# Decode attention with a gated MLP on one core: wo in another place of the key ring, the last loads placed and divided anew, exponentials put before copies

## The chip, the cores and the metric

The kernel runs on one core of a Trainium2 chip. The core has a matrix engine (PE, with its weight loads shown as PEld), a vector engine (DVE), a scalar engine (ACT), GpSimd (POOL) and a queue for loads (SP). Each of them works through its own list of instructions in order. Loads from memory (HBM) go through 16 DMA engines, which share out every load among them. The metric is the time of one execution on the device in microseconds (us).

## The reference

For a batch of 4 with one new token each, a layer norm of x feeds two branches, and their sum with x is the output (4 x 1 x 640, bf16).

```python
xn = layernorm(x)                                  # x: 4 x 1 x 640
q = (xn @ wq)                                      # 32 heads of 128
scores = einsum('bhqd,bhkd->bhqk', q, k_cache) * 128 ** -0.5
o = einsum('bhqk,bhkd->bhqd', softmax(scores), v_cache)   # 4096 keys
A = o.reshape(4, 1, 32 * 128) @ wo
z = gelu(xn @ w_in); z1, z2 = z[..., :864], layernorm(z[..., 864:])
B = (z1 * (w_sp * z2 + b_sp)) @ w_out
out = x + A + B
```

Each of the 4 x 32 heads has its own 4096 keys and values of 128 numbers. These two caches are nearly all of the 282 MB that are read.

## The kernel before

The attention is cut into 16 *units*. A unit `u` is 8 heads of one batch row: `hg, b = divmod(u, 4)`; four units make a group `hg`, which ends with a projection by 8 heads' rows of `wo` (1.31 MB). The keys of a unit are 8.39 MB, and so are its values. In on-chip memory they lie over 128 partitions, 16 partitions to a head.

**Places.** Keys live in a ring of seven places of 2.1 MB each (`ring`), four places to a unit. Units with an even number use places 3 to 6, odd ones 0 to 3 (`k_at`, L128); `k_order` (L129) says in which order a unit's four quarters are worked on, so that an odd unit begins with place 3. Values have one room of their own, `v_all`, for one unit. The exceptions are at the end: units 14 and 15 have their own places (L130, L131), the last unit's values go into places 0 to 3 of the ring when these are free (`VE_AT`), and `wo` of each group goes into one ring place (`WO_AT`, L132).

**Steps.** The loop over `n = 4 u + i` takes one quarter of keys per step:

- `product` (L487, DVE) multiplies the quarter by the unit's query, in place; `fold_half` (L493, DVE) adds its two halves.
- `sums` (L502, PE) adds further by 8 matmuls with an identity into PSUM; `row_sums` (L515, DVE) of the step before ends it. When `sums` is issued the place is given free (`busy.remove`, L509).
- In the first step of the next unit come `head_max` (L524 to L531, DVE: the maximum), `exps` (L537, ACT: the exponentials, with their sums) and `by_head` (L548, DVE: spreads them to a matrix `p_m` with zeros for the other heads).
- `weighted` (L572, PE, 64 matmuls) multiplies `p_m` by the values into `pv`; `take` (L584, ACT) copies `pv` to `o_rows`; `picked` (L603 or, in the last group, L650, PE) adds the rows that belong together.
- `weighted` and `take` of unit u stand in the second step of unit u+1 (`turns`, L662), of units 12 and 13 in the fourth step of the next unit (L663, L664); unit 14's comes after the loop.
- After a group: `group_turn` (DVE) and `group_proj` (L633, PE), which gives wo's place free.

**The loads' list.** `loads` (L167 to L175) is one list in a fixed order, each entry with the places it needs. `pump`, called at the end of every step, issues entries from the head of the list as long as their places are free, and stops at the first that isn't. SP then still waits, in order, for the engines that last read the place. So an entry whose place comes free late also holds all the entries behind it. In the middle the order is values of u, keys of u+2, and after every fourth unit wo; the end is (keys in halves):

```python
loads += [k_load(NU - 2, 0, 2), v_load(NU - 4), k_load(NU - 2, 2, 4), k_load(NU - 1, 0, 2)]
loads += [v_load(NU - 3), k_load(NU - 1, 2, 4), v_load(NU - 2)]
loads += [ve_load(0, (0, NC)), ve_load(1, V_CUTS), wo_load(HG - 1)]
```

The last unit's values come as one load for the first half and four of falling size for the second (`V_CUTS`), the last wo in five parts.

**The end.** After the loop: `weighted` and `take` of unit 14, the last row sums, maximum, `exps` and `by_head` of unit 15; the sum of the exponentials (L717); picks of unit 14; `weighted` of unit 15's first half; its copy and picks; 128 small matmuls (L732) for the second half; the division (L740), the projection by the last wo (L633), a copy (L746) and the store.

The order on PE, DVE, ACT and SP is the order in which the program issues the instructions. In this text K14 means the keys of unit 14, V14 its values, wo2 the wo of group 2.

Of the kernel before, what the change touches and what calls it, by code (L numbers as in the profile page):

```python
# [17 lines left out]
def kernel(  # L18
# [14 lines left out]
    nc = tc.nc  # L33
# [19 lines left out]
    NU = HG * Bsz  # L53
    NR = HT * S // P
    NK = 4
    HC = NR // NK
    NC = 2 * HC
    HD2 = Dh // 2
    RW = 8
    QW = HC * Dh  # L60
# [6 lines left out]
    NG = NR // CB  # L67
# [25 lines left out]
    v_all = places.tile([P, NK * QW], BF16, name="v_all")  # L93
# [22 lines left out]
    def run_of(cache, u):  # L116
        hg, b = divmod(u, Bsz)
        return cache[b, HT * hg : HT * (hg + 1)].rearrange("h s d -> (h s) d").rearrange(
            "(p c) d -> p (c d)", c=NR
        )  # L120
# [5 lines left out]
    k_at, k_order = {}, {}  # L126
    for u in range(NU):
        k_at[u] = [r if u % 2 else NK - 1 + r for r in range(NK)]  # L128
        k_order[u] = [NK - 1, 0, 1, 2] if u % 2 else [0, 1, 2, 3]  # L129
    k_at[NU - 2], k_order[NU - 2] = [4, 5, 0, 1], [0, 1, 2, 3]  # L130
    k_at[NU - 1], k_order[NU - 1] = [2, 3, 4, 5], [0, 1, 2, 3]  # L131
    VE_AT, WO_AT = (0, 2), 6  # L132

    def k_load(u, r0=0, r1=NK):
        at = k_at[u][r0:r1]

        def go():
            nc.sync.dma_start(
                out=ring[:, at[0] : at[0] + r1 - r0, :],
                in_=run_of(A_k_cache, u)[:, r0 * QW : r1 * QW].rearrange("p (r w) -> p r w", w=QW),  # L140
            )

        return go, at

    def v_load(u):
        def go():
            nc.sync.dma_start(out=v_all[:], in_=run_of(A_v_cache, u))

        return go, [V]

# [16 lines left out]
    loads = [k_load(0, 0, 2), (load_w, []), k_load(0, 2, 4), k_load(1)]  # L167
# [3 lines left out]
            loads.append(wo_load(u // Bsz))  # L171
    assert u + 2 == NU - 3
    loads += [k_load(NU - 2, 0, 2), v_load(NU - 4), k_load(NU - 2, 2, 4), k_load(NU - 1, 0, 2)]
    loads += [v_load(NU - 3), k_load(NU - 1, 2, 4), v_load(NU - 2)]
    loads += [ve_load(0, (0, NC)), ve_load(1, V_CUTS), wo_load(HG - 1)]  # L175
    busy = {V}
    n_loaded = [0]
# [10 lines left out]
    v_runs = v_all[:].rearrange("p (c d) -> p c d", d=Dh)  # L188
# [24 lines left out]
    for e in range(PAR):  # L213
        nc.gpsimd.tensor_copy(
            out=of_row[:, e, :, :, e, :],
            in_=ident[:].rearrange("p (k q) -> p q k", q=QD)[:, 0:Bsz, :, None].to_broadcast(
                [P, Bsz, NQ, LN]
            ),
# [15 lines left out]
    for i in range(NSTAT):  # L234
# [5 lines left out]
        out=rstd[:], in_=mv[:, 1:2], func=ACT.Sqrt, bias=eps_tile[:Bsz], scale=1.0  # L240
# [4 lines left out]
        out=xn_bf[:],  # L245
# [9 lines left out]
    for c in range(DC):  # L255
        nc.tensor.transpose(
            out=xnT_ps[:, c, :], in_=xn_v[:, c, :], identity=ident[:Bsz, :Bsz]
# [8 lines left out]
    for e in range(PAR):  # L266
        q_ps = ps_pv.tile([P, HG, Dh], FP32, tag="pv", name="q_ps")
        for c in range(DC):
            for k in range(NQ):
                nc.tensor.matmul(  # L270
                    out=q_ps[k * QD : (k + 1) * QD],
# [7 lines left out]
            out=rows[:], in0=q_ps[:], scalar1=scale_qk, scalar2=None, op0=ALU.mult  # L279
# [7 lines left out]
        out=hot[:].rearrange("p c h -> p (c h)"),  # L287
        in_=ident[:].rearrange("p (g m) -> p m g", m=QD),
# [6 lines left out]
        out=pick[:, :, Bsz - 1 :].rearrange("p c (k q) -> p c k q", q=QD)[  # L295
            :, :, :, 0 : PAR * Bsz : Bsz
        ],
# [236 lines left out]
    def exps(u):  # L534
        hg, b = divmod(u, Bsz)
        p_c[u] = small.tile([P, NR], BF16, name="p_c")
        nc.scalar.activation(  # L537
            out=p_c[u][:],
            in_=scores.pop(u)[:],
            func=ACT.Exp,  # L540
            bias=maxes.pop(u)[:],
            scale=1.0,
            accum_out=row_den[hg % NACC][:, b : b + 1],
        )

    def by_head(u):
        hg, b = divmod(u, Bsz)
        nc.vector.tensor_tensor(  # L548
            out=p_m[:, u % 2],
            in0=p_c.pop(u)[:].rearrange("p (g c) -> p g c", c=CB)[:, :, :, None].to_broadcast(  # L550
                [P, NG, CB, HT]
            ),
            in1=own[:, None, None, :].to_broadcast([P, NG, CB, HT]),
            op=ALU.mult,
        )
        if b == Bsz - 1:
            nc.vector.tensor_tensor(
                out=acc[hg % NACC][:, :, 0 : PAR * Bsz].rearrange("p k (e b) -> p k e b", b=Bsz),
                in0=row_den[hg % NACC][:, None, None, :].to_broadcast([P, NQ, PAR, Bsz]),
                in1=own[:].rearrange("p (e k) -> p k e", e=PAR)[:, :, :, None].to_broadcast(  # L560
                    [P, NQ, PAR, Bsz]
                ),
                op=ALU.mult,
            )

    def weighted(u, v_at, g0=0, more=False):
        n_g = v_at.shape[1] // CB
        if g0 == 0:
            pvs[u] = ps_pv.tile([P, GW], FP32, tag="pv", name="pv")
        for n in range(n_g):  # L570
            cg = n % CB
            nc.tensor.matmul(  # L572
                out=pvs[u][cg * QD : (cg + 1) * QD, :],
                lhsT=p_m[:, u % 2, g0 + n].rearrange("p c h -> p (c h)"),
                rhs=v_at[:, n * CB : (n + 1) * CB, :],
                start=(g0 == 0 and n < CB),
                stop=(not more and n >= n_g - CB),
            )
# [3 lines left out]
    def take(u):  # L582
        o = taken[u] = small.tile([P, CB, Dh], FP32, name="o_rows")
        nc.scalar.copy(out=o[:].rearrange("p c d -> p (c d)"), in_=pvs.pop(u)[:])  # L584
# [73 lines left out]
    def picked(u):  # L658
        (pick_last if u // Bsz == HG - 1 else pick_unit)(u)
# [7 lines left out]
    with tc.manual_schedule(engines={E.PE, E.DVE, E.Activation, E.SP}):  # L667
        stage_q(0)
        waiting = None
        mlp = gmlp()  # L670
        for n in range(NK * NU):
            u, i = divmod(n, NK)
            product(n)
            if n in (1, 2):
                next(mlp)
            if n:
                row_sums(n - 1)
            if i == 0 and u:
                head_max(u - 1)
                if waiting is not None:  # L680
                    picked(waiting)
            fold_half(n)
            if n == 1:
                next(mlp)
            if n in (1, 2):
                next(mlp)
            if i == 0 and u:
                exps(u - 1)
                by_head(u - 1)
            sums(n)  # L690
            if i == 0 and u + 1 < NU:
                stage_q(u + 1)
            if i == 0 and waiting is not None:
                if waiting % Bsz == Bsz - 1:
                    group_turn(waiting // Bsz)
                    group_proj(waiting // Bsz)
                waiting = None
            if n == 0:
                next(mlp)
            if n == 2:  # L700
                busy.remove(V)
            if n in turns:
                w = waiting = turns[n]
                if w % Bsz == Bsz - 1:
                    group_den(w // Bsz)
                weighted(w, v_runs)
                take(w)
                busy.remove(V)
            pump()
        weighted(NU - 2, v_runs)  # L710
        take(NU - 2)
        row_sums(NK * NU - 1)
        head_max(NU - 1)
        exps(NU - 1)
        by_head(NU - 1)
        den = ps_m.tile([P, NQ, PAR, Bsz], FP32, tag="m", name="den_all")
        nc.tensor.matmul(  # L717
            out=den[:],
            lhsT=ones_sq[:],
            rhs=acc[(HG - 1) % NACC][:, :, 0 : PAR * Bsz],  # L720
            start=True,
            stop=True,
        )
        rden = small.tile([P, NQ, PAR, Bsz], FP32, name="rden_all")
        nc.vector.reciprocal(out=rden[:], in_=den[:])
        picked(NU - 2)
        u, b = NU - 1, Bsz - 1
        weighted(u, v_ends[0])
        take(u)
        pick_last(u, more=True)  # L730
        for c in range(NC):
            nc.tensor.matmul(  # L732
                out=o_last[0][:, :, :, b],
                lhsT=v_ends[1][:, c, :],
                rhs=p_m[:, u % 2, NG // 2 + c // CB, c % CB, :].rearrange("p (e k) -> p k e", e=PAR),
                start=False,
                stop=(c == NC - 1),
            )
        o_n = small.tile([P, NQ, PAR, Bsz], BF16, name="o_n_last")
        nc.vector.tensor_tensor(out=o_n[:], in0=o_last[0][:], in1=rden[:], op=ALU.mult)  # L740
        gr[HG - 1] = [o_n[:, h % NQ, h // NQ, :] for h in range(HT)]
        group_proj(HG - 1)

        res = work.tile([P, NOH], BF16, name="res")
        out_v = out.flatten_outer_dims()
        nc.scalar.copy(out=res[0 : OG + Bsz], in_=out_ps[0 : OG + Bsz])  # L746
        nc.scalar.dma_start(out=out_v[:, 0:NOH], in_=res[0:Bsz])
        nc.sync.dma_start(out=out_v[:, NOH:D], in_=res[OG : OG + Bsz])
# [30 lines left out]
```

## Time and profile before

| what | us |
|---|---|
| median of three timed executions | 670.37 (669.91 to 671.1) |
| the profiled execution, its own time | 668.77 |
| span from its first to its last instruction | 667.0 |
| DVE busy | 522.5 (78%) |
| PE busy | 310.5 (47%) |
| ACT busy | 29.5 (4%) |
| DMA in the chain of waits | 61% of the span |
| mean granted clock of PE | 0.698 |
| read from memory | 282.24 MB, 423 GB/s over the span |

The page cuts the span into 40 slices and shows for each how busy every engine was, the granted clock of PE, the busy share of the DMA engines and the GB/s that they moved. The chain of waits follows the work that ended last back from the end: each line is a start, a length, and what it was (an engine and a line of the kernel, or a load in flight). The timeline of a queue shows when each load was issued. The table of windows gives busy time by engine for chosen stretches. The trace also keeps, for each load, a mark from every DMA engine that took part when its share was complete.

### The profile page before, as it was taken

Reading aid. Unit: us, or ns where it says so; the run is one execution under the profiler, and the core shown is the slowest. Engines: PE = TensorE matmul, PEld = TensorE weight load, DVE = VectorE, ACT = ScalarE, POOL = GpSimd, SP = SyncE. Lnnn points to the kernel's source line nnn. Section 1 sums busy time; section 2 is a strip of 40 time slices with the busy share of each in tenths; the row PEclk is TensorE's granted clock in tenths of the full one; section 3 lists DMA queues with packets and bytes.
Section 4 is the critical chain, followed back from the end, with each engine's and each line's share of the span. In section 5 each row is a group of like instructions: output and inputs, shape, how many; then the busy total and the mean of one; then the engine's idle time right before and its main releaser. Section 6 shows DMA issues by size and latency. Waiting matters only on the chain.

```text
span 667.0 us, 4615 instructions
## 1 busy us (share of the span) xinstructions
PE 310.5 (47%) x1999; PEld 136.1 (20%) x1999; DVE 522.5 (78%) x325; ACT 29.5 (4%) x73; POOL 2.7 (0%) x12
## 2 busy tenths in 40 slices
PE   0365372526336253552735255252653734646357
PEld 0131121112213121220212112021221311212125
DVE  2578978959697894969879596795969789997950
ACT  0020000000000000000000000000000000000000
POOL 1000000000000000000000000000000000000000
PEclk9756676766768686576767668576576866767685
DMA  9999999999999999999999999999999999999995
GB/s 376 421 465 436 425 429 421 433 440 440 429 436 402 451 432 432 437 436 436 433 429 422 409 424 441 436 437 436 436 437 436 405 436 398 415 459 436 401 414 221
DMA packets 8128, 282.54 MB, mean 424 GB/s; under 512 B 832, under 2 KB 1964, under 8 KB 3116
## 3 DMA queue, kind: packets, MB, share of 16 engines
q1 hardware_dynamic: 8088, 282.24, 98.5%
q8 instruction: 15, 0.25, 0.1%
q14 instruction: 5, 0.04, 0.0%
q10 hardware_dynamic: 20, 0.01, 0.0%
HBM read 282.24 MB, written 0.01 MB: 423 GB/s over the span
## 4 chain that ended last, share of the span: by engine, by line
DMA 61%; DVE 25%; PE 12%; issue 1%; ACT 0%; SPq 0%; DVEq 0%; ACTq 0%
DMA k_ring<-in_A_k_cache_dram 56%; DVE k_ring L487 13%; PE s_ps L502 7%; DVE k_ring L493 7%; DMA v_all<-in_A_v_cache_dram 5%; PE pv L572 3%; DVE s_sb L515 2%; DVE p_m L548 1%; DVE m L524 1%; PE out_ps L633 1%; PE o_last L650 1%; PE o_last L732 1%; DVE mt L526 0%; DVE mt L529 0%; DVE nm L531 0%
## 5 line engine op out<-in xcount | busy, mean ns | idle before, releaser
L487 DVE TENSOR_TENSOR k_ring<-k_ring,qbc 128x8192 bf16<-128x8192 bf16 x64 | 282.8, 4419 | 91.6 <-DMA k_ring<-in_A_k_cache_dram 91.6
L502 PE MATMUL s_ps<-k_ring,ident 128*128 128x512 bf16 x512 | 199.9, 561 | 316.4 <-DVE k_ring L493 316.3
L502 PEld LDWEIGHTS <-ident 128*128 128x128 bf16 x512 | 65.3, 130 | 429.7 <-issue 381.5
L493 DVE TENSOR_TENSOR k_ring<-k_ring 128x4096 bf16<-128x4096 bf16 x64 | 146.0, 2282 | 0.0
L572 PE MATMUL pv<-v_all,p_m 128*32 128x512 bf16 x960 | 60.5, 409 | 4.7 <-DMA v_all<-in_A_v_cache_dram 4.7
L515 DVE TENSOR_REDUCE s_sb<-s_ps 128x64 f32<-128x512 f32 x64 | 43.8, 684 | 4.2 <-PE s_ps L502 4.2
L548 DVE TENSOR_TENSOR p_m<-p_c,own 128x2048 bf16<-128x2048 bf16 x16 | 36.6, 2286 | 8.6 <-ACT p_c L537 8.6
L572 PEld LDWEIGHTS <-p_m 128*32 128x32 bf16 x992 | 26.6, 104 | 42.8 <-issue 19.7
L584 ACT COPY o_rows<-pv 128x512 f32<-128x512 f32 x16 | 9.4, 586 | 258.5 <-PE pv L572 258.5
L603 PEld LDWEIGHTS o_ps<-o_rows,pick 128*128 128x128 f32 x96 | 19.4, 280 | 4.1 <-issue 3.0
L537 ACT ACTIVATE p_c<-s_sb,nm 128x256 bf16<-128x256 f32 x16 | 8.1, 508 | 250.0 <-DVE nm L531 250.0
L603 PE MATMUL o_ps<-o_rows,pick 128*128 128x128 f32 x96 | 18.3, 355 | 0.0
L278 DVE TENSOR_SCALAR q_rows<-q_ps 128x512 bf16<-128x512 f32 x2 | 1.4, 692 | 14.3 <-PE q_ps L270 14.3
L270 PE MATMUL q_ps<-v_all,xnT 128*32 128x512 bf16 x40 | 4.5, 630 | 11.0 <-DMA v_all<-in_A_wq_dram 11.0
L477 ACT CAST qbc<-qbc_ps 128x128 bf16<-128x128 f32 x16 | 4.3, 266 | 104.7 <-PE qbc_ps L469 104.7
L740 DVE TENSOR_TENSOR o_n_last<-o_last,rden_all 128x32 bf16<-128x32 f32 x1 | 0.2, 192 | 10.9 <-PE o_last L732 10.9
L524 DVE TENSOR_REDUCE m<-s_sb 128x1 f32<-128x256 f32 x16 | 6.7, 420 | 0.6
L650 PE MATMUL o_last<-hot,o_rows 128*128 128x8 f32 x32 | 5.8, 310 | 2.2 <-ACT o_rows L584 2.2
L469 PE MATMUL qbc_ps<-q_rows,of_row 128*128 128x128 bf16 x32 | 6.2, 284 | 0.6 <-DVE q_rows L278 0.6
L650 PEld LDWEIGHTS o_last<-hot,o_rows 128*128 128x128 f32 x32 | 5.5, 261 | 4.1 <-ACT o_rows L584 4.1
L469 PEld LDWEIGHTS <-of_row 128*128 128x128 bf16 x32 | 4.2, 135 | 8.3 <-issue 7.7
L633 PE MATMUL out_ps<-k_ring,o_t 128*4 128x320 bf16 x48 | 5.2, 378 | 0.1
(87 smaller groups left out, 69.7 us busy)
## 6 DMA issues: line engine op xcount, KB each, us to landing
k_ring<-in_A_k_cache_dram SPq DMA_DIRECT2D x6, 4096.0 KB, 20.1
v_all<-in_A_wq_dram SPq DMA_DIRECT2D x1, 5120.0 KB, 15.5
k_ring<-in_A_v_cache_dram SPq DMA_DIRECT2D x1, 4096.0 KB, 34.2
k_ring<-in_A_wo_dram SPq DMA_DIRECT2D x3, 1280.0 KB, 6.2
v_all<-in_B_w_in_dram SPq DMA_DIRECT2D x1, 2160.0 KB, 29.4
k_ring<-in_A_v_cache_dram SPq DMA_DIRECT2D x1, 2048.0 KB, 36.4
k_ring<-in_A_v_cache_dram SPq DMA_DIRECT2D x1, 1024.0 KB
k_ring<-in_A_v_cache_dram SPq DMA_DIRECT2D x2, 512.0 KB
```

The costliest lines, as they stand in the source:

```text
L469: nc.tensor.matmul(out=qb_ps[:], lhsT=of_row[:, e, b].rearrange("p k f l -> p (k f l)"), rhs=q_rows[e][:, hg, :], start=(e == 0), stop=(e ...
L487: nc.vector.tensor_tensor(out=t, in0=t, in1=qbcs[u][:, None, :].to_broadcast([P, HC, Dh]), op=ALU.mult)
L493: nc.vector.tensor_tensor(out=t[:, :, 0:HD2], in0=t[:, :, 0:HD2], in1=t[:, :, HD2:Dh], op=ALU.add)
L502: nc.tensor.matmul(out=s[:], lhsT=ident[:], rhs=t[:, :, g * RW : (g + 1) * RW], start=(g == 0), stop=(g == m - 1),)
L515: nc.vector.tensor_reduce(out=scores[u][:, r * HC : (r + 1) * HC], in_=sums_ps.pop(n)[:], axis=AX.X, op=ALU.add,)
L524: nc.vector.tensor_reduce(out=m1[:], in_=scores[u][:], axis=AX.X, op=ALU.max)
L548: nc.vector.tensor_tensor(out=p_m[:, u % 2], in0=p_c.pop(u)[:].rearrange("p (g c) -> p g c", c=CB)[:, :, :, None].to_broadcast([P, NG, CB, HT]
L572: nc.tensor.matmul(out=pvs[u][cg * QD : (cg + 1) * QD, :], lhsT=p_m[:, u % 2, g0 + n].rearrange("p c h -> p (c h)"), rhs=v_at[:, n * CB : ...
L584: nc.scalar.copy(out=o[:].rearrange("p c d -> p (c d)"), in_=pvs.pop(u)[:])
L603: nc.tensor.matmul(out=gr[hg][:], lhsT=pick[:, c, Bsz - 1 - b : P + Bsz - 1 - b], rhs=o[:, c, :], start=(b == 0 and c == 0), stop=(b == Bs ...
L633: nc.tensor.matmul(out=out_sum(half), lhsT=o, rhs=wo_sb[:, n, half * NOH : (half + 1) * NOH], start=False, stop=(hg == HG - 1 and n == HT ...
L650: nc.tensor.matmul(out=o_last[0][:, :, :, u % Bsz], lhsT=o[:, c, :], rhs=hot[:, c, :].rearrange("p (e k) -> p k e", e=PAR), start=(c == 0) ...
```

## The change

- wo lies in the ring's fifth place (number 4) and not in its seventh (number 6).
- The keys of unit 14 lie in places 5, 6, 0, 1 and not 4, 5, 0, 1; those of unit 15 in 2, 3, 5, 6 and not 2, 3, 4, 5. Unit 13 works through its places from 0 to 3, where it began with 3.
- The values of unit 13 come in two loads of half the size, and `weighted` of unit 13 in two calls of 32 matmuls, one for each half.
- For units 12, 13 and 14 the copy `take` is put behind the `exps` of the unit after, on ACT, and the picks that use it behind the `sums` of that step, on PE (for unit 14, which comes after the loop, only the copy moves).

```diff
-    k_at[NU - 2], k_order[NU - 2] = [4, 5, 0, 1], [0, 1, 2, 3]
-    k_at[NU - 1], k_order[NU - 1] = [2, 3, 4, 5], [0, 1, 2, 3]
-    VE_AT, WO_AT = (0, 2), 6
+    k_order[NU - 3] = [0, 1, 2, 3]
+    k_at[NU - 2], k_order[NU - 2] = [5, 6, 0, 1], [0, 1, 2, 3]
+    k_at[NU - 1], k_order[NU - 1] = [2, 3, 5, 6], [0, 1, 2, 3]
+    VE_AT, WO_AT = (0, 2), 4
...
-    def v_load(u):
+    def v_load(u, r0=0, r1=NK):
+        part = slice(r0 * QW, r1 * QW)
+
         def go():
-            nc.sync.dma_start(out=v_all[:], in_=run_of(A_v_cache, u))
+            nc.sync.dma_start(out=v_all[:, part], in_=run_of(A_v_cache, u)[:, part])
...
-    loads += [v_load(NU - 3), k_load(NU - 1, 2, 4), v_load(NU - 2)]
+    loads += [v_load(NU - 3, 0, 2), (v_load(NU - 3, 2, 4)[0], []), k_load(NU - 1, 2, 4), v_load(NU - 2)]
...
             if i == 0 and u:
                 head_max(u - 1)
-                if waiting is not None:
+                if waiting in taken:
                     picked(waiting)
             fold_half(n)
...
             if i == 0 and u:
                 exps(u - 1)
+                if waiting in pvs:
+                    take(waiting)
                 by_head(u - 1)
             sums(n)
             if i == 0 and u + 1 < NU:
                 stage_q(u + 1)
             if i == 0 and waiting is not None:
+                if waiting in taken:
+                    picked(waiting)
                 if waiting % Bsz == Bsz - 1:
...
-                weighted(w, v_runs)
-                take(w)
+                if w == NU - 3:
+                    weighted(w, v_runs[:, 0:NC], more=True)
+                    weighted(w, v_runs[:, NC:NR], NG // 2)
+                else:
+                    weighted(w, v_runs)
+                if i < NK - 1:
+                    take(w)
                 busy.remove(V)
             pump()
         weighted(NU - 2, v_runs)
-        take(NU - 2)
         row_sums(NK * NU - 1)
         head_max(NU - 1)
         exps(NU - 1)
+        take(NU - 2)
         by_head(NU - 1)
```

## The prediction, made before the result was known

> **What bounds the kernel now.** I read the page's slices and queues first, then the chain of waits, then the loads' own queue in order of time, and last a table of windows over the end.
>
> ```profile
> span 667.0 us, 4615 instructions
> DMA  9999999999999999999999999999999999999995
> GB/s 376 421 465 436 425 429 421 433 440 440 429 436 402 451 432 432 437 436 436 433 429 422 409 424 441 436 437 436 436 437 436 405 436 398 415 459 436 401 414 221
> q1 hardware_dynamic: 8088, 282.24, 98.5%
> q8 instruction: 15, 0.25, 0.1%
> ```
>
> The 16 DMA engines are busy nearly all the time. The loads' queue carries 282.24 MB. In the steady part 16.78 MB (keys and values of one unit) pass every 38.6 us (102.48 to 141.08 in the chain), so 8.39 MB take 19.30 us, 434.6 GB/s. So only three things can change the time: stretches where a DMA engine has nothing queued, an engine that runs late, and what remains after the last byte. Slices 13, 23, 32, 34, 38 and 40 are clearly below their neighbours. The last line is instructions read by the same engines, 15 pages of 16 KB.
>
> ```profile
> 44.00:200.00 156.00, 71.66 (x376) 29.05 (x377) 132.47 (x87) 6.97 (x18) 0.00 (x0) 0.69 1.01 436
> 526.00:542.00 16.00, 4.46 (x16) 2.56 (x16) 9.35 (x7) 0.00 (x0) 0.00 (x0) 0.74 0.98 406
> 560.00:572.00 12.00, 5.95 (x14) 1.97 (x14) 12.00 (x6) 0.00 (x0) 0.00 (x0) 0.50 0.88 364
> 660.00:667.00 7.00, 3.88 (x76) 2.38 (x72) 0.19 (x1) 0.42 (x1) 0.00 (x0) 0.50 0.03 9
> ```
>
> The last columns are granted clock, DMA share and GB/s. From 560 to 572 some 2 us of full rate are missing, (436-364) x 12 / 436; the last 7 us move nothing.
>
> ```profile
> 533.07 0.38 SPq L202 DMA_DIRECT2D k_ring<-in_A_wo_dram  x1
> 566.09 7.46 SPq L138 DMA_DIRECT2D k_ring<-in_A_k_cache_dram  x2
> 591.73 0.33 SPq L138 DMA_DIRECT2D k_ring<-in_A_k_cache_dram  x1
> 614.02 0.33 SPq L147 DMA_DIRECT2D v_all<-in_A_v_cache_dram  x1
> ```
>
> These are issues late against the queue: wo of group 2, the second keys of unit 14 (566.09), the values of unit 14 (614.02). And the end, from the chain:
>
> ```profile
> 577.47 31.19 DMA v_all<-in_A_v_cache_dram
> 608.71 5.30 PE pv L572 x59
> 614.12 0.44 issue
> 614.56 0.61 ACT p_c L537 x2
> 615.19 2.29 DVE p_m L548
> ...
> 642.15 3.92 PE pv L572 x34
> 646.19 0.44 issue
> 646.63 0.61 ACT p_c L537 x2
> 647.26 2.29 DVE p_m L548
> ...
> 661.87 2.31 PE out_ps L633 x16
> 664.21 0.42 ACT res L746
> ```
>
> Twice the exponential (p_c) starts only after the copy of pv, although its input, the maximum on DVE, was done at 608.43 and 644.02. From 642 to the end it is a chain on PE, ACT and DVE, not DMA.
>
> The trace also keeps a completion mark for each of a DMA's 16 engines; the first and the last mark tell how early the leading engine and how late the last one is. Loads land in issue order. Last marks: K13 536.22, wo2 539.29, K14's first half 548.97, V12 568.92, K14's second 579.02, K15's first 588.68, V13 608.66, K15's second 618.42, V14 637.95, V15's first half 649.11, its four smaller parts 653.96, 656.41, 657.65, 658.90, wo3's five parts 659.66 to 662.11. At 434.6 GB/s the 52.95 MB after K13 need 121.8 us; they took 125.9.
>
> **The change part by part.**
>
> *Exponentials ahead of the copies, and the end.* In the tail exps(15) starts when its maximum is there. How early is that? At the loop's step 60 exps(14) no longer waits for the pv of unit 13: by_head(14) follows fold_half (ends 610.56) at once and not at 615.19. DVE then runs on: by_head 2.2 to 612.8, product 4.4 to 617.1, row sums 0.6, fold 2.2 to 619.9 (K15's second half has landed at 618.42), product, sums, fold to 627.1, product, sums, fold to 634.3; PE sums 3.6 to 637.9; row sums and maximum (642.18 to 644.02) to 639.8; exponential and by_head to 642.8. That is 6.7 us before 649.5 today. Meanwhile pv of unit 14 waits for V14 (637.95) and takes 4 us; its copy and picks end at about 645.5. Then PE must wait for V15's first half, 649.11, where today it comes to it at 651.94. From there by today's rows: 32 pv matmuls 3.56 to 652.7, copy 0.6 to 653.3, picks 1.9 to 655.2, 128 small matmuls at 28 ns, paced by the last marks: 64 to 657.0, 32 to 657.9, 16 to 658.3, the last 16 behind 658.90 to 659.4. o_n_last to 659.7. The projection (0.144 per matmul) is paced by wo3's marks: the last head lands at 662.11, its two matmuls end at about 662.8, where L633 ends today at 664.2. So -1.35 with the DMAs unmoved. What hid it is gone: behind this, the last byte decides. Bounds: 0, if the last head's part lands later by as much, to -1.7, if only its landing counts.
>
> *First half of K14's second load.* Unit 13 takes its places from 0 on, so places 0 and 1 are free after its second step, not its third: the issue moves by one step of 7.1 us, from 566.09 to about 559. V12's engines were done from 567.18 on (first mark), and an issue needs over a microsecond to reach them. Against 9.65 us for 4.19 MB, its last mark came after 10.10 and its first after 10.38: -0.45 on the late engine, -0.73 on the leading. The end goes by the late one: -0.45; bounds 0 and -0.73. K15's halves are issued as before (places 2, 3 after unit 13's last step; 5, 6 after unit 14's second).
>
> *Values of unit 13 in halves.* PE's first 32 matmuls no longer wait for the second half; V14 is issued when the last 32 are done, 608.66 + 2.7 = 611.4 instead of 614.02. Now V14's last mark comes 19.52 us after K15's, its first 19.90 after: -0.2 (bounds 0 and -0.6). SP's queue: K15's second half, V15's parts and wo3 stand behind it and are issued no later. The extra DMA: halves K14b and K15a land 9.66 apart, a whole load 19.30, so +0.02; upper bound the 0.04 by which V15's small parts (1.25 for 1.21) exceed their bytes. The Trainium skill (DMA: Bandwidth & Descriptors, Anatomy of one DMA) fits about 2.0 us fixed plus bytes over 436 GB/s per DMA, for the GpSimd path; by that rule the half adds 2.0 and the sum would be -1.0. The 9.66 us row, with the next load queued, speaks against it.
>
> *wo in place 4.* Place 4 is free after an even unit's second step, place 6 after its fourth, so wo0, wo1, wo2 and the V4, V8 behind them in SP's order are issued some 10 us earlier (a values load without wo goes 13 us after its keys: 204.7, not 215.12). K6 and K10 still wait for the projection (231.57) as today, since wo's place, 4 or 6, lies in theirs. Cover for wo0 to wo2 themselves: nobody needs them before the projection. On the marks wo0 took 3.26, wo1 4.63, wo2 3.07 on the late engine, 3.83, 3.98 and 4.62 on the leading one; 3.02 would be its bytes. Taking 3.07 as undisturbed, the late engine can gain 0.2 at wo0 and 0 to 1.56 at wo1. I can't tell whether wo1's 1.56 is a late issue (373.40, first engine done about 374) or a slow engine, so I take half, -0.8. wo3 is free early in both.
>
> *Picks and row order.* PE takes sums(56) and sums(60) before the picks; row sums have 4 us of cover on DVE. Nothing; at worst one pick group, 1.06 us, ahead of a DMA issue that has 14 us.
>
> Sum: -1.35 -0.45 -0.2 +0.0 -0.2 -0.8 = -3.0. The profiled execution took 668.77 (span 667.0 and 1.77 around); the three timed ones have a median of 670.37, 1.6 above it and none as low. Carried over: 665.8 profiled, 667.4 as a median. What a measurement here can tell from nothing is about 0.2%, 1.3 us.
>
> **Rivals.**
>
> *Only the end gains.* The empty stretches hit only leading engines, which wait for the late one anyhow: wo2's late engine lost nothing. Then -1.35: 669.0.
>
> *Leaders absorb more.* Most losses on the last marks (V12 +0.64, V13 +0.69, V15's first half +1.5) fall where a 16 KB page of instructions was read on one DMA engine. If leading engines keep the lead that they lose today at wo2 and K14 (1.6 and 0.73), half of these 2.8 disappear: 666.0.
>
> *A fixed cost per DMA*, as weighed above, at the divided load: -3.0 + 2.0: 669.4.
>
> *The change doesn't shorten the end.* SP held an issue of wo3 for 8.1 us (637.96) and another for 3.6 behind a full queue. If the fuller queue holds wo3's last parts back by 1.5 us or more, the end stands still and the rest of the gain is lost in it: 670.2. Against it: today the last part is issued at 653.98, eight microseconds ahead of landing.
>
> *Slower: one late engine.* The end is the slowest of 16 engines. If instruction pages and wo's packets keep falling on the engine that is already last, it loses again what the leaders gain: four or five pages at 0.64 to 1.5 make 4.6 us against 3.0, 672.0; it decides from 4.3 on. For it: the lag grew from 1.1 us (wo2) to 3.2 (V15). Against: of the 14 pages read from 90 us on only some four moved the last mark.
>
> **How the numbers follow.** The forecast 0.50; only the end 0.17; leaders 0.13; fixed cost 0.05; no shorter end 0.07; late engine 0.08. Faster: 0.50 + 0.13 + half of 0.17 (669.0 lies on the border) = 0.72; same 0.09 + 0.05 + 0.07 = 0.20, slower 0.08. The forecast's own range is 665.9 (all upper bounds, -4.4) to 669.0; with the other cases 664.9 to 669.8.
>
> **What would show it.** Right: the second K14 issue near 559, V14's near 611; exps ahead of o_rows in steps 56, 60 and at the end; PE waiting for V15's DMA before its last pv; the last wo landing about 660.5 and res 0.7 us behind. Wrong: wo issues near 204 and 363 with wo1's late mark still 4.6 after K9's; a last landing at 662 or later; two halves of V13 over 9.7 us apart.

## The result, and the profile after

The changed kernel takes 662.93 us (median of four executions, 662.39 to 663.45) against 670.74 (669.91 to 671.6) for the kernel before in the same comparison: 0.9883 of the time, 95% interval 0.9866 to 0.9901, 7.8 us less. The forecast was 667.4, 3.0 us less, in a range of 664.9 to 669.8. The sign was right and the size was not. Medians here and below are over all executions of a comparison; the ratios leave out the few that took 6 to 24 us more than the median of their kernel.

The profiled execution of the changed kernel took 662.98, right at its median. That of the kernel before took 668.77, 2 us under the median of its timed ones. So the two traces show 5.8 of the 7.8 us; where the other 2 are is told below.

From the page of the changed kernel, the span and the slices:

```profile
span 661.2 us, 4618 instructions
DMA  9999999999999999999999999999999999999996
GB/s 377 424 459 408 437 441 440 433 444 428 413 444 436 441 424 428 441 428 440 437 437 421 425 444 437 432 432 437 424 437 444 428 430 427 413 437 425 460 399 277
```

The bytes are the same, and the dip of slice 34 (398 before, at 550 to 567 us) is a 427 now. Single slices still differ from their neighbours by some 30 GB/s; the marks below are finer. The windows over the two stretches where the queue had run low:

```profile
526.00:542.00 16.00, 5.28 (x16) 3.03 (x16) 9.31 (x10) 0.35 (x1) 0.00 (x0) 0.66 0.97 418
560.00:572.00 12.00, 6.71 (x16) 2.16 (x15) 12.00 (x5) 0.00 (x0) 0.00 (x0) 0.72 0.95 410
```

They move 418 and 410 GB/s where it was 406 and 364. The end of the chain of waits:

```profile
608.76 26.27 DMA v_all<-in_A_v_cache_dram
635.05 21.96 DMA k_ring<-in_A_wo_dram
657.01 0.04 issue
657.06 1.27 PE out_ps L636 x8
658.35 0.42 ACT res L758
```

From the issue of V14 (608.76) to the landing of the last wo but two parts (657.01), the chain is loads alone. Before, its last 22 us (642 to 664) were PE, ACT and DVE. Why is seen on ACT and PE, in order of time:

```profile
606.71 0.51 ACT L540 ACTIVATE p_c<-s_sb,nm 128x256 bf16<-128x256 f32 x1 [27.38 <-DVE nm L534]
608.77 0.59 ACT L587 COPY o_rows<-pv 128x512 f32<-128x512 f32 x1 [1.46 <-PE pv L575]
638.01 0.51 ACT L540 ACTIVATE p_c<-s_sb,nm 128x256 bf16<-128x256 f32 x1 [28.66 <-DVE nm L534]
640.13 0.59 ACT L587 COPY o_rows<-pv 128x512 f32<-128x512 f32 x1 [1.52 <-PE pv L575]
```

```profile
644.75 3.60 PE L575 MATMUL pv<-k_ring,p_m 128*32 128x512 bf16 x32 [2.37 <-DMA k_ring<-in_A_v_cache_dram]
654.57 0.60 PE L744 MATMUL o_last<-p_m,k_ring 128*128 128x8 bf16 x16 [0.61 <-DMA k_ring<-in_A_v_cache_dram]
```

The exponentials start behind the maximum (in brackets: idle time and who ended it), and the copies come after. PE waits 2.37 us for V15's first half and 0.61 for its last part, where it had come late to both. The store's copy starts 0.51 us after the last landing (657.84), before it was 2.1 us after it (662.11 to 664.21). So in the two traces 1.6 us come from the end and 4.3 from an earlier last byte (662.11 to 657.84).

### The profile page after: what moved, and what is told of

Read it like the earlier page. It is cut to its first block, busy times and chain, and to the rows that moved or that the text cites. A ratio compares the mean times of both kernels' runs of the same rounds, so it can differ in the third digit from the quotient of the medians.

```text
span 661.2 us, 4618 instructions
## 1 busy us (share of the span) xinstructions
PE 305.8 (46%) x1999; PEld 133.8 (20%) x1999; DVE 522.3 (79%) x325; ACT 29.8 (5%) x73; POOL 2.6 (0%) x12
## 4 chain that ended last, share of the span: by engine, by line
DMA 64%; DVE 26%; PE 9%; issue 1%; ACT 0%; SPq 0%; DVEq 0%
DMA k_ring<-in_A_k_cache_dram 57%; DVE k_ring L490 14%; PE s_ps L505 7%; DVE k_ring L496 7%; DMA v_all<-in_A_v_cache_dram 4%; DMA k_ring<-in_A_wo_dram 3%; DVE s_sb L518 2%; DVE m L527 1%; PE pv L575 1%; DVE p_m L551 1%; PE out_ps L636 1%; DVE mt L529 0%; DVE mt L532 0%; DVE nm L534 0%; DVE o_n L618 0%
## 5 line engine op out<-in xcount | busy, mean ns | idle before, releaser
L505 PEld LDWEIGHTS <-ident 128*128 128x128 bf16 x512 | 65.4, 129 | 434.6 <-issue 385.8
L575 PE MATMUL pv<-v_all,p_m 128*32 128x512 bf16 x960 | 59.1, 402 | 0.2 <-DMA v_all<-in_A_v_cache_dram 0.2
L575 PE MATMUL pv<-k_ring,p_m 128*32 128x512 bf16 x32 | 3.6, 631 | 2.4 <-DMA k_ring<-in_A_v_cache_dram 2.4
```

The costliest lines, as they stand in the source:

```text
L505: nc.tensor.matmul(out=s[:], lhsT=ident[:], rhs=t[:, :, g * RW : (g + 1) * RW], start=(g == 0), stop=(g == m - 1),)
L575: nc.tensor.matmul(out=pvs[u][cg * QD : (cg + 1) * QD, :], lhsT=p_m[:, u % 2, g0 + n].rearrange("p c h -> p (c h)"), rhs=v_at[:, n * CB : ...
```

## Where the earlier last byte comes from: each part alone, and each part undone

The completion marks, from the trace, of wo and of the other loads on which the two kernels differ most (K14a and K14b are the first and the second load of K14, and so on; V15a is the first half of V15); "first" and "last" are the first and the last of the 16 DMA engines, each counted from its mark of the load before (us):

```
               kernel before      changed kernel
               first    last      first    last
K2 (19.30*)    19.29   19.30      19.28   20.11
wo0 (3.02*)     3.83    3.26       3.10    3.06
K9 (19.30*)    19.31   20.08      19.32   19.33
wo1 (3.02*)     3.99    4.63       3.09    3.11
K10 (19.30*)   19.32   19.32      19.32   20.07
K11 (19.30*)   19.32   19.30      19.32   20.10
wo2 (3.02*)     4.62    3.07       3.09    3.03
V12 (19.30*)   19.31   19.94      19.33   19.35
K14b (9.65*)   10.38   10.10       9.67    9.68
K15a (9.65*)    9.68    9.66      10.68    9.65
V13 (19.30*)   19.34   19.99      19.35   19.40   (two halves)
V14 (19.30*)   19.91   19.52      19.37   19.31
V15a (9.65*)    9.68   11.16       9.67    9.67
* its bytes at 434.6 GB/s
```

Over all loads the 4.3 us on the last engine are wo 1.8, K14b 0.4 and V14 0.2; 1.1 net at jumps that fall on a read of a page of instructions (before at K9, V12, V13 and V15a, after at K2, K10 and K11; what a page costs is measured below); and 0.8 in small differences, 0.5 of it already at the second half of K0, ahead of anything that the change touches. One load goes out late now that did not before: K15a, at 572.23 (573.22 before), now 1.0 us ahead of the leading engine's mark, where it was 4.3. The leading engine loses 1.0 there, the last one nothing.

**Queue or chain.** Theory one, the queue: the gain is DMA engines that no longer run out of queued work. Its rival, the chain: the gain is the shorter compute chain at the end. Each part alone on the kernel before, then each part taken back from the changed kernel.

Places alone:

```diff
-    k_at[NU - 2], k_order[NU - 2] = [4, 5, 0, 1], [0, 1, 2, 3]
-    k_at[NU - 1], k_order[NU - 1] = [2, 3, 4, 5], [0, 1, 2, 3]
-    VE_AT, WO_AT = (0, 2), 6
+    k_at[NU - 2], k_order[NU - 2] = [5, 6, 0, 1], [0, 1, 2, 3]
+    k_at[NU - 1], k_order[NU - 1] = [2, 3, 5, 6], [0, 1, 2, 3]
+    VE_AT, WO_AT = (0, 2), 4
```

> The kernel before with wo in place 4 and the places of units 14 and 15 that follow from it, nothing else. Queue theory (the gain is DMA engines that no longer run out of queued work): -2 to -4 us, wo1's last mark 3.1 us behind K9's and not 4.6, leading engines without a gap at wo0, wo1, wo2 (first marks 3.0 to 3.1 apart, not 3.8 to 4.6). Chain theory (the gain is the shorter compute chain at the end): 0 to -1 us, because the exponentials still wait for the copies.

Unit 13's order alone (`+    k_order[NU - 3] = [0, 1, 2, 3]`):

> The kernel before with unit 13 worked from place 0 on, nothing else. Both theories: the second keys of unit 14 are issued at about 559 and not 566. Queue theory: -0.5 to -1 us. Chain theory: 0, the values of unit 13 decide the chain.

The two halves of V13 alone (the hunks on `v_load`, `loads` and `weighted` of the diff above):

> The kernel before with the values of unit 13 in two loads and their matmuls in two calls, nothing else. Chain theory: the 5.3 us of matmuls behind the landing become 2.6, so everything behind moves by 2.6 us until the last landing stops it: -1.4 to -2.6 us. Queue theory: -0.2 us (the values of unit 14 issued 2.6 us earlier, a gap of 0.2 on the late engine). A fixed cost per DMA of 2 us would give +0.6 to +2.

The exponentials ahead of the copies alone (the hunks on `picked`, `take` and `exps`):

> The kernel before with exponentials ahead of the copies and the picks moved, nothing else. Chain theory: -1.4 to -1.9 us, the end then waits for the last landing (first pv matmul of unit 15 right behind its load). Queue theory: at most -1.4 us from the end, and the last landing where it was (about 662 in the profiled execution).

The same four, undone in the changed kernel:

> The changed kernel with wo back in place 6 and the old places of units 14 and 15. Queue theory: +2 to +4 us against the changed kernel, with the gaps of the leading engines back at each wo and wo1's last mark 4 us or more behind K9's. Chain theory: 0 to +0.5.

> The changed kernel with unit 13 beginning with place 3 again. The second keys of unit 14 are issued at about 565, 2 us behind the leading engines' end of the load before. Queue theory: +0.4 to +1.5 us. If only the late engine counts, 0, since it ends 3.8 us after the leading one there.

> The changed kernel with the values of unit 13 in one load again. The values of unit 14 are issued at about 611.5 and not 608.8, the exponentials still don't wait: 0 to +0.5 us by both theories. A fixed cost per DMA would show as -2.

> The changed kernel with the copies ahead of the exponentials again and the picks where they were. Chain theory by its rows: by_head of unit 14 1.4 us later, exps(15) behind the copy of unit 14 at about 642.8, pv of unit 15 begins at 647 and not 644.75: +0.9 us (0.5 to 2). Queue theory: 0.

Measured, as the ratio to the kernel before of the same comparison (median 671.8 for the first four, 671.9 for the second) with its interval, and as a median:

| part | alone | undone |
|---|---|---|
| places (wo in 4) | 0.9909 (0.9874 to 0.9944), 667.68 | 0.9943 (0.9922 to 0.9963), 667.48 |
| unit 13's order | 0.9978 (0.9955 to 1.0001), 670.09 | 0.9877 (0.9857 to 0.9898), 663.94 |
| V13 in halves | 0.9947 (0.9918 to 0.9976), 668.66 | 0.9860 (0.9839 to 0.9880), 662.85 |
| exponentials first | 0.9957 (0.9934 to 0.9980), 668.69 | 0.9860 (0.9840 to 0.9881), 662.73 |

Undoing the places costs 4.6 us (667.48 - 662.93), and alone they give 4.1 (671.82 - 667.68): a little beyond the queue theory's 2 to 4, and far from the chain theory's 0.5 and 1. (By the ratio e1 gives 6.1, interval 3.8 to 8.5.) Undoing the order costs 1.0, as the queue theory had it; alone it can't be told from nothing. Undoing the halves or the exponentials costs nothing, though alone each gives some 3 us (e3 -3.2, e4 -3.1 by medians, more than either theory allowed, 2.6 and 1.9; but the intervals, 1.6 to 5.5 and 1.3 to 4.4 us, hold these values too). My chain reading of u4, +0.9, was wrong.

**Do the halves and the exponentials stand in for each other?** Both undone in the changed kernel, and both alone on the kernel before:

> The changed kernel with the values of unit 13 in one load and the copies ahead of the exponentials: the places and unit 13's order alone remain. Each of the two undone alone changed nothing (662.85 and 662.73). If they stand in for each other, the chain through the pv of unit 13 comes back: +1.5 to +3 us. If neither matters: 0.

> The kernel before with the halves and the exponentials ahead of the copies, wo in place 6 and all places as before. Alone they gave 0.9947 and 0.9957 of the time before. If they stand in for each other: -3 to -4 us together. If they add: -6.5.

They do. Without both the changed kernel takes 665.65, +2.7; together on the kernel before they give 668.48 against 672.17 (0.9963, 0.9939 to 0.9988), hardly more than either alone. The costs of undoing, places 4.6, order 1.0 and these two together 2.7, add up to 8.3, of 7.8 measured. The label of the first says "order", but it is the order of exponentials and copies that is undone there; unit 13's order is kept. With both undone, the chain ends as before:

```profile
642.94 0.44 issue
643.38 0.61 ACT p_c L538 x2
644.01 2.29 DVE p_m L549
...
648.76 3.56 PE pv L573 x26
...
658.61 2.31 PE out_ps L634 x16
660.95 0.42 ACT res L747
```

In u3 (one load for V13, exponentials first) the pv of unit 13 takes its full time behind the landing and V14 is issued 2.1 us later, at 610.83, and still nothing is lost at the end, since the leading DMA engine is done with the load before only at 612.83:

```profile
575.17 30.55 DMA v_all<-in_A_v_cache_dram
605.73 0.04 issue
605.77 5.04 PE pv L573 x64
610.83 24.19 DMA v_all<-in_A_v_cache_dram
635.03 21.99 DMA k_ring<-in_A_wo_dram
```

## What a late issue costs

The marks give the places' share a cause to test. In seven profiles in which wo is issued late (before, e2, e3, e4, e5, u1 and w3 below), its last mark comes 3.04 to 6.12 us after that of the keys, 4.32 on average over 21 loads; in ten with an early issue, over 12 us ahead, it is 3.02 to 3.12 in every case. "Late" is by the issue against the leading engine's mark of the load before: 1.5 us or less ahead of it. This distance is called the lead below. As issued in u1:

```profile
215.05 0.38 SPq L205 DMA_DIRECT2D k_ring<-in_A_wo_dram  x1
374.05 0.38 SPq L205 DMA_DIRECT2D k_ring<-in_A_wo_dram  x1
534.09 0.38 SPq L205 DMA_DIRECT2D k_ring<-in_A_wo_dram  x1
```

The leading engine's marks there are 216.13, 375.40 and 533.92, and wo takes 4.92, 3.18 and 5.43 on the last one. The packets show it too: wo goes in 256 packets of 5 KB, each 0.196 us and 50.2 us in all when it is queued early (changed kernel: no packet over 0.20), but 56.5, 58.4 and 58.3 us in all in the kernel before, with single packets of 0.90 to 1.62. From issue to the first packet pass 1.03 to 1.05 us (214.68 to 215.73, 373.40 to 374.44, 533.07 to 534.10).

But place and lateness go together in all of these. To part them I held wo back with the places as changed. First in the order of the program alone:

```diff
-        return (lambda: load_wo(hg)), [WO_AT]
+        return (lambda: load_wo(hg)), [WO_AT] + ([HOLD] if hg < HG - 1 else [])
...
+            if i == NK - 1:
+                busy.discard(HOLD)
             pump()
+            busy.add(HOLD)
```

> The changed kernel, wo still in place 4, but its load for groups 0 to 2 held back to the fourth step of the unit, where the kernel before issued it. If the late issue is what costs: the last engine takes 4 to 5 us for most of the wo loads (mean 4.2 in five profiles with late issues, against 3.05 with early ones), packets of wo that last up to 1 us and not 0.20, +3.5 us (2 to 5) in all. If the place or the order of the keys is what counts: 0.

662.48 us, and this said nothing: SP still issued wo at 200.67. The step in which `pump` calls a load sets its rank on SP; when SP issues it is set by what it must wait for, and place 4 was free. So next a real wait:

```diff
+        nc.sync.dma_start(out=ring[0:1, RING - 1, 0:2], in_=A_x.flatten_outer_dims()[0:1, 0:2])
         nc.sync.dma_start(
             out=wo_sb.rearrange("p (e j) n -> p e j n", e=PAR),
```

> The changed kernel, wo in place 4, but a load of four bytes ahead of each wo of groups 0 to 2 on SP that must wait for the fourth step's sums (it writes into place 6, and nothing reads it). So wo is issued where the kernel before issued it, this time by a real wait. Late issue costs: +3.5 us (2 to 5) against the changed kernel, last marks of wo at 4 to 5 us, wo packets of up to 1 us. Place costs: 0 to +0.3.

663.5 us. The four bytes meet only what the first of eight matmuls reads, so wo went out 2.9, 3.2 and 1.7 us ahead of the leading engine's marks, and its last marks stayed at 3.07, 3.12 and 3.02; only the leading engine lost 0.3 at the third. (The profiled execution took 668.39, the other five 662.4 to 664.0; its last engine lost 2.4, 1.3 and 1.0 us at K1, V0 and K2, ahead of the first wo.) Waiting for the last matmul instead (`56:58` for `0:2`):

> As w2_wo_waits, but the four bytes go to where the last of the eight matmuls of the fourth step's sums reads, not the first, so SP waits some 3 us longer (w2 issued wo 3.2 us ahead of the leading engine's end mark at wo0 and wo1, 1.7 at wo2, and its wo loads lost nothing on the last engine). Then wo goes out 0.5 to 1.5 us ahead of that mark, as in the kernel before. Late issue costs: +2 to +5 us, last marks of wo 4 to 5 us for most. Place costs: 0.

```profile
215.38 0.39 SPq L207 DMA_DIRECT2D k_ring<-in_A_wo_dram  x1
374.34 0.38 SPq L207 DMA_DIRECT2D k_ring<-in_A_wo_dram  x1
535.12 0.38 SPq L207 DMA_DIRECT2D k_ring<-in_A_wo_dram  x1
```

668.5 us (0.9973, 0.9947 to 0.9999), +5.8 against the changed kernel's 662.69 of the session before, with every place as changed. The leads are 0.6, 1.1 and -0.6 us, the last marks 4.17, 6.12 and 4.18. It is the late issue, not the place. Why the last mark moves as well stays open: at wo1 of the kernel before, the engine that ended K9 last was busy until 377.05, 3.65 us after wo's issue and 2.6 after its first packet, and still the last mark came 1.6 us late. The trace does not say which engine ended wo last.

Is that wo's short rows? The same two waits ahead of six values loads, with rows of 64 KB:

```diff
+        late = u in (5, 6, 7, 9, 10, 11)
         def go():
+            if late:
+                at = k_at[u][k_order[u][NK - 1]]
+                nc.sync.dma_start(out=ring[0:1, at, 0:2], in_=A_x.flatten_outer_dims()[0:1, 0:2])
             nc.sync.dma_start(out=v_all[:, part], in_=run_of(A_v_cache, u)[:, part])
```

> The changed kernel with the same four-byte load ahead of the values of units 5, 6, 7, 9, 10 and 11, so that these six loads are issued some 10 us later, about when the leading DMA engine has finished the load before. If any load that finds an empty queue costs a start of about 1 us: leading engines lose 1 us at each, the last one 0 to 1.4, so +4 to +8 us. If only wo's short rows suffer: 0 to +1.

> As v1_values_wait with the same 3 us more, so that the six values loads go out about when the leading engine ends (v1 had leads of 2.1 to 5.5 us and lost at most 0.34 on the leading engine and nothing on the last). If a start from an empty queue costs any load: +3 to +8 us. If only wo's short rows suffer: 0 to +1, leading engines alone lose.

> The changed kernel as it is, for a second profile and as the measure for the other two on the same chip: 662.5 to 663.5 us, wo's last marks 3.0 to 3.1 us behind those of the keys.

The changed kernel again: 662.69, wo's last marks 3.04 each. With leads of 2.1 to 5.5 us (v1) nothing is lost, 662.77. With the longer wait 667.05 (0.9938, 0.9917 to 0.9959), +4.4. Its two latest in the profile:

```profile
295.81 0.33 SPq L156 DMA_DIRECT2D v_all<-in_A_v_cache_dram  x1
455.36 0.33 SPq L156 DMA_DIRECT2D v_all<-in_A_v_cache_dram  x1
```

They go 0.5 and 0.6 us ahead of the leading marks (296.34, 455.96). The leading engine takes 20.72 and 20.60 for them and not 19.31, the last one 21.17 and 19.69. The other four have leads of 2.2 to 2.6 and lose at most 0.5 on the leading engine. So it is not wo's short rows alone: the values loads pay too. But not every late load pays on the last engine (nothing at K15a of the changed kernel, lead 1.0). Over all the profiles, leads of 1.5 us and less cost the last engine 0 to 3.1 us. Leads between 1.5 and 3 us cost it 0.2 at most, with two exceptions that I can't explain: K14b in e4 (lead 1.8) and in e3 (1.9), 1.9 and 1.2 us. The leading engine begins to lose at 2.0 to 2.3 (0.8 in u3).

**What the late engine is late for.** The jumps of K9, V12, V13 and V15a before (0.8, 0.6, 0.7, 1.5) and of K2, K10 and K11 after (0.8 each) in the table of marks come where a page of PE's instructions was read. To see the price of a page, 128 small matmuls more ahead of the sums of two steps in units 1 to 11:

```diff
+        if 1 <= u <= NU - 5 and n % NK >= 2:
+            for _ in range(P):
+                nc.tensor.matmul(
+                    out=s[:, 0, :], lhsT=ident[:], rhs=ident[:, 0:RW], start=True, stop=True
+                )
         for g in range(m):
```

> The changed kernel with 128 small matmuls more ahead of the sums of the third and fourth step of units 1 to 11 (their result is overwritten by the sums; 22 pages of 16 KB of instructions more, PE has the idle time). If each page costs the DMA engine that reads it 0.6 to 0.8 us and they go round the 16 engines: +1 to +2 us. If they always come by the same engine: +13 or more. If pages are free and the late engine is late for another reason: 0.

```profile
span 666.0 us, 10261 instructions
PE 391.8 (59%) x4815; PEld 207.0 (31%) x4815; DVE 523.2 (79%) x325; ACT 29.8 (4%) x73; POOL 2.6 (0%) x12
q8 instruction: 37, 0.61, 0.3%
```

667.8 us, +4.9, more than I had worked out: 0.22 us for each of 22 pages. The last mark jumps by 1.56 to 1.58 us at K4, K7, K10 and V11, twice a page's 0.7 to 0.8 each time, 6.3 us in all, so the late engine gets more than its sixteenth of the pages. That pages go round unevenly is read from these marks; the trace does not name the engine of a packet. PE was 59% busy, and some issues were late: at K9, K11, K14a and K15a the leading engine lost 0.9, 1.2, 1.0 and 2.1 us (leads 2.1, 1.5, 1.6 and -0.1), but the last one 0.1 at most, so the 4.9 us don't come from there.

## Why the prediction was wrong

- **The step that failed is the term for wo in place 4.** It stood in the sum as -0.2 - 0.8 = -1.0. In the two traces it is 1.8; in medians undoing the places costs 4.6 us, and making wo late again with the places kept 5.8. The mechanism was named (the late issue, the leading engines without work), and the question was put whether wo1's 1.56 us was a late issue or a slow engine; it was the late issue. The size failed because it was read from one profiled execution in which two of three wo loads happened to lose almost nothing on the last engine (3.26, 4.63, 3.07, together 1.8 over 3 x 3.05; six other profiles with late issues have 3.3 to 5.3, and all seven 3.8 on average). Taking wo2's 3.07 as "undisturbed" hid that others pay 2 us there (u1 2.4, e2 2.2). The first marks had it: 3.83, 3.99 and 4.62 in that same trace, and I set them aside because the end goes by the last engine.
- **The carried-over 1.6 us failed too.** The forecast kept the distance between the profiled execution and the median (665.8 and 667.4). In the changed kernel there is none: 662.98 and 662.93.
- **The range.** Its upper bounds were summed as -4.4, which takes V13's at 0.2; with the stated 0.6 they make -4.8, or 665.6, still 2.7 us above the measured time.
- **The scatter of the timed executions was a sign, and I read past it.** The profiled execution lay under all three timed ones. In the later comparisons the kernel before ranges from 667.3 to 677.6 us; the changed kernel and u3, u4 stay within about 1 us. The kernels with a late wo scatter like the kernel before (u1 664.8 to 671.8, w3 665.9 to 673.2). But e1, with wo early and K14b late, does too (663.9 to 672.2), while u2, with K14b as late, does not (663.7 to 664.2, four executions): what makes the scatter is not settled. The 2 us by which the traces and the medians differ lie within the scatter of the kernel before.
- **"Only the end gains"** (0.17): wrong, 4.3 of the 5.8 us in the traces are an earlier last byte. It rested on wo2's last mark.
- **"Leaders absorb more"** (0.13): the saving is there, the reason isn't shown. The losses on V12, V13 and V15a (0.64, 0.69 and 1.5) are gone to within 0.1, though pages are still read at 552.5, 597.7 and 639.6 us. But the changed kernel loses 0.8 each at the pages of K2, K10 and K11, the kernel before 0.8 at that of K9, so 1.1 us net are left, near the 1.4 that the rival counted. Which engines read which page may be chance: the trace does not name them. The first and the last engine are 3.9 us apart behind K13 and 2.6 at the end; 1.0 of this went at K15a, where the leading engine ran dry.
- **The end, -1.35:** the mechanism right, its place in the sum not. In the traces the end gives 1.6 us. The worked chain fits: pv of unit 15 waits for its load, the projection is paced by wo3's parts, res 0.5 us behind the last byte (forecast 0.7). But I gave the credit to the exponentials alone. They can go back without loss while the halves are there, and the halves while the exponentials are first; both undone cost 2.7.
- **K14's second load, -0.45:** 0.42 in the traces (10.10 to 9.68), issue 558.02 (forecast 559); undoing costs 1.0 in medians. Right mechanism, half the size: in u2 the load goes out 0.7 us behind the leading engine's mark, that engine loses 2.6 us (12.27 for 9.65), the last one 0.7. "K15's halves are issued as before" did not hold against the queue: K15a kept its time within 1 us while the loads ahead of it moved by 2 on the last engine and 4 on the first.
- **V13 in halves, -0.2 and +0.02:** V14 was issued at 608.76 (forecast 611.4, since V13 landed earlier too) and V14's gap is gone. The halves land 9.67 and 9.73 apart, so the divided load has no price while others are queued. The Trainium skill's 2.0 us fixed per DMA (DMA: Bandwidth & Descriptors, Anatomy of one DMA), given for the GpSimd path, does not show there. What a load pays that finds the queue all but empty, 0 to 3.1 us on the last engine and 1.3 on average for wo, is another quantity, and no run shows whether it has the same source. I weighed a price for a load that was queued and too small a one for the three that weren't.
- **Slower through one late engine, no shorter end:** neither happened. SP was held at wo3's issues again (the five stretch over 27.66 us from 623.12), and the last part still landed in its turn, 0.41 us behind the one before.

## What to carry to other kernels

When loads bound a kernel, read for every load how far ahead of the leading DMA engine's end it is issued: here a lead of 2 us cost the slowest engine 0.2 us at most, and 1.5 us or less cost it 0 to 3 us. Free the place of a small load early, for it holds every load behind it in the queue. And take the price of an event that occurs three times in an execution from more than one execution: if the timed ones scatter more than the profiled one's place among them explains, the events themselves may be scattering.

## What the runs showed that was not expected

- Pages of instructions have a price in a kernel bound by loads. 22 pages of 16 KB cost 4.9 us here, though their bytes (0.36 MB) are worth 0.8 us at 434.6 GB/s, and 6.3 us of jumps on the last mark come where pages were read. The likely reason, argued from the packets (0.9 to 1.0 us for a page's 16 KB) and not shown engine by engine, is that each page falls on one engine and the slowest engine counts. The Trainium skill (Runtime: NRT & Kernel Launch, Instruction fetch mechanics) calls the crossing of a page mostly hidden; for the engine that executes them that may hold, for the loads it does not here (0.22 us a page).
- Two parts that gave some 3 us each alone gave hardly more together, and either could be dropped from the changed kernel. A sum over parts would have counted them twice; only undoing both showed their worth.
- The order in which a program calls its loads and the time at which the queue issues them are two things: holding a call back by two steps (w1) changed nothing at all.
